# Another order of work in the opening of a fused attention and feed-forward kernel

## The chip, the cores and the metric

The kernel runs on one core of one Trainium2 chip. A core has five engines with their own instruction queues: TensorE (PE: matmuls, and the loading of their weights as PEld), VectorE (DVE), ScalarE (ACT), GpSimd (POOL) and SyncE (SP, which here only issues DMAs); POOL and ACT issue DMAs too. Each engine takes its instructions strictly in order and waits on semaphores for the others. The metric is the device time of one execution in microseconds (us).

## The reference

The reference is attention over four batches, eight heads, 768 positions and 64 numbers a head, followed by a feed-forward network (FFN) with a maximum over three products. Five of the heads keep only the first four keys and a window of 64 keys ("streaming" heads), three keep all keys up to the position ("retrieval" heads); which ones is an input.

```
scores = scale * q @ k.T                       # per batch and head, 768 x 768
mask   = causal                if is_retrieval[h]
         causal & (sink|window) otherwise
a      = softmax(where(mask, scores, -1e9))
x      = (a @ v), heads side by side           # 3072 x 512
h      = max(max(x @ w1, x @ w2), x @ w3)      # 512 -> 768
out    = h @ w_out                             # 768 -> 512
```

## The kernel before

**Units of work.** A batch is cut into two halves of 384 query rows, and its heads, in the order `HEADS`, into two groups of four. One tile `t` is one half and one group: `t = 4*batch + 2*half + group`. A tile has two pairs of heads, `i` = 0 and 1. The FFN is cut into 21 units for each half batch: 18 sums (three weights by six blocks of 128 columns, each four matmuls of 384 columns) and three output blocks.

**An order written out by hand.** No scheduler orders the instructions. Three long lists of items, `FIRST` (line 62), `NEAR` (line 75) and `ANY` (line 118), are read from left to right, and each item calls one function (the table `do`, near the end of the kernel function) that puts its instructions on the queues of the engines concerned. What stands earlier in a list stands earlier on every queue that it uses. `FIRST` is the opening: it ends with `av`s and transposes of batch 0's first half. Then a branch on the input flags takes `NEAR` where the retrieval heads are the ones that the kernel knows, or `ANY` where they are others; with this input it is `NEAR` (its masks `NM`, line 565, are in the trace, and only `NEAR` makes them).

**The items that matter here.** The last letter names the engine of a copy: `a` ACT, `d` DVE, `p` POOL.
- `hl half pair n which s`: SP loads a pair of heads of batch 0's k (which = 0) or q (1) in a half. `load_v`: loads v. SP's list of DMAs is in one order before and after.
- `cast half pair which e` (line 335): turns such a load to 16 bit, into one of three buffers `kn` or `qn`.
- `turnp half pair ee` (lines 362 and 378): PE transposes six blocks of 128 columns into one or two PSUM banks; the named engines copy them to the tile `KQ`.
- `em pair`: two DVE instructions (line 599) that write the mask of two heads, for the early scores; `flags` and `read` bring the flags into place, `far` the factors of distant keys.
- `s t u [i]`: scores. PE adds the mask (line 851, in tiles 0 and 1) and the products (line 876) into a score buffer `st` (two of them) or, with `b`, into two banks, and ACT takes the exponential (line 887) into `pt`.
- `v t i e` (line 730) casts v; `vp half n e` (lines 747 and 750) puts its rows in order by three matmuls of 512 columns and a copy; `vf` (line 762) scales it.
- `av t i` (lines 964, 977 and 979): the product with v into a bank; DVE takes the reciprocal of the sums and writes `x`. `x t i e` (lines 998 and 1002) transposes it for the FFN as `xT`.
- `w 0 2 part`: POOL issues three DMAs (line 619) with half of the weight w1 (the tile `w0t`). `load b g`: POOL issues four DMAs (line 389) with k and q of a batch; `turn b g which part` (line 407) is a DVE transpose of a quarter of that load.
- `f 1 e`: the next FFN unit, with its copy, if it has one, on engine `e`; maxima are always on DVE (line 673).
- `idle n`: PE computes n empty products of 512 columns (line 484) into a score buffer that nobody reads. `number`: each engine reads the branch flag (line 1061).
- `k`, `c`, `kc`: masks on `pt` after the exponential, and joins of the first keys with the window's.

**Buffers.** There are four PSUM banks of the general kind, taken in turn by `turnp`, `vp`, `av`, `x`, `f` and by scores with `b`; the fifth user waits until the first one's bank is read. There are two `st`, taken in turn. The lines that decide this:

```
sps = turns("sps", 2, space=bass.MemoryType.PSUM)
bkp = turns("bkp", 4, space=bass.MemoryType.PSUM)

def run(program):
    for line in program:
        for item in line.split(", "):
            name, *args = item.split()
            do[name](*args)
```

Of the kernel before, what the change touches and what calls it, by code (L numbers as in the profile page):

```python
# [59 lines left out]


FIRST = (
# [10 lines left out]
)  # L73
# [42 lines left out]
)  # L116

ANY = (
# [1029 lines left out]
```

## Time and profile before

| | before |
|---|---|
| time, median of 3 runs | 189.58 us (189.18 to 189.71) |
| the profiled execution's own time | 190.51 us |
| its span | 188.7 us |
| PE busy | 181.1 us (96%) |
| DVE, ACT, POOL busy | 140.3 (74%), 103.6 (55%), 85.7 us (45%) |
| first FFN matmul of a real unit | 23.05 us after the span's start |
| PE's longest wait after that | 0.73 us, at 76.8 us |

A busy share is the time in which an engine has an instruction under way. In the timeline each row has the start, the time that the row covers, the engine, the line, the operation, its tiles and how many instructions were merged (x3); in brackets stands how long the engine had been idle and what ended the wait. "bank" is any of the four PSUM banks. PE's rows start when the first matmul of the group enters, and matmuls overlap: successive ones of 384 columns start some 0.16 us apart at the full clock.

### The profile page before, as it was taken

To read this page: it belongs to the slowest core of one execution; us is meant where nothing else is said; L and a number is where in the kernel's file an instruction comes from. 1 tells how busy PE (TensorE), PEld (TensorE's weight loads), DVE (VectorE), ACT (ScalarE), POOL (GpSimd) and SP (SyncE) were. 2 spreads that over 40 slices of the span, in tenths; PEclk is the share of its full clock that TensorE was granted. 3 is DMA by queue.
4 is the path that set the end of the run, shared out by engine and by line. 5 is a ranking of instruction groups with operands and counts; after the bars stand their busy time and mean duration, and the time that the engine had idled before them with its cause. 6 is when DMAs were issued, how large, how long until landed. Compare 5 with 4: busy or idle time off the path is not lost. (4 is left out here: it accounts for less than half of the span.)

```text
span 188.7 us, 4937 instructions
## 1 busy us (share of the span) xinstructions
PE 181.1 (96%) x1930; PEld 104.6 (55%) x1930; DVE 140.3 (74%) x297; ACT 103.6 (55%) x164; POOL 85.7 (45%) x121
## 2 busy tenths in 40 slices
PE   7989999999999999799999999999999999999992
PEld 2446646555565555375556565664656456746552
DVE  3739999999869996999899868773658357834740
ACT  4488999442676994548585548545245534123022
POOL 6258989600569797069302286059922402000000
PEclk9999999999999999999999999999999999999998
DMA  4999999995999999972999541211212220332004
GB/s 129 266 349 280 171 196 209 205 202 118 227 184 246 183 198 229 247 63 53 206 259 192 91 167 24 42 26 67 105 21 45 86 102 2 66 95 94 7 0 167
DMA packets 43180, 26.49 MB, mean 140 GB/s; under 512 B 30866, under 2 KB 38674, under 8 KB 43154
## 3 DMA queue, kind: packets, MB, share of 16 engines
q1 hardware_dynamic: 37794, 18.03, 39.3%
q0 software_dynamic: 4944, 7.87, 24.7%
q8 instruction: 15, 0.25, 0.5%
q10 hardware_dynamic: 416, 0.26, 0.4%
q14 instruction: 11, 0.09, 0.2%
HBM read 25.17 MB, written 6.29 MB: 167 GB/s over the span
## 5 line engine op out<-in xcount | busy, mean ns | idle before, releaser
L887 ACT ACTIVATE pt<-st 128x1024 f16<-128x1024 f32 (+2 forms) x72 | 63.0, 927 | 27.9 <-PE st L876 22.8
L648 PE MATMUL bank<-xT,w1t 128*128 128x384 f16 x180 | 35.7, 326 | 0.7 <-DVE acc L673 0.7
L648 PE MATMUL bank<-xT,w2t 128*128 128x384 f16 x180 | 36.0, 326 | 0.0
L673 DVE TENSOR_TENSOR acc<-bank,acc 128x384 f16<-128x384 f32 x45 | 24.9, 556 | 14.9 <-PE bank L648 12.4
L648 PE MATMUL bank<-xT,w0t 128*128 128x384 f16 x180 | 35.7, 326 | 0.2 <-DVE hT L673 0.2
L908 POOL TENSOR_TENSOR pt<-pt,NM 128x1024 f16<-128x1024 f16 (+2 forms) x14 | 26.6, 1910 | 11.2 <-ACT pt L887 10.4
L668 ACT CAST acc<-bank 128x384 f16<-128x384 f32 x33 | 15.5, 485 | 29.2 <-PE bank L648 28.8
L692 PE MATMUL bank<-woutt,hT 128*128 128x512 f16 (+1 forms) x138 | 30.7, 372 | 0.0
L673 DVE TENSOR_TENSOR hT<-bank,acc 128x384 f16<-128x384 f32 x45 | 24.5, 556 | 4.7 <-PE bank L648 2.1
L407 DVE STREAM_TRANSPOSE KQ<-kq 128x384 f32<-128x384 f32 x24 | 25.8, 1129 | 1.6 <-DMA kq<-in_k_dram 1.6
L648 PEld LDWEIGHTS <-w0t 128*128 128x128 f16 x192 | 17.9, 98 | 12.9 <-issue 1.3
L648 PEld LDWEIGHTS <-w1t 128*128 128x128 f16 x192 | 17.6, 98 | 12.5 <-issue 1.3
L926 POOL TENSOR_TENSOR pt<-pt,mk 128x512 f16<-128x512 f16 (+1 forms) x12 | 12.9, 1080 | 25.2 <-ACT pt L887 24.7
L648 PEld LDWEIGHTS <-w2t 128*128 128x128 f16 x192 | 17.4, 98 | 11.2 <-issue 0.4
L692 PEld LDWEIGHTS <-hT 128*128 128x128 f16 x156 | 14.4, 98 | 15.4 <-issue 0.3
L964 PEld LDWEIGHTS <-pt 128*128 128x128 f16 x492 | 18.6, 97 | 4.2 <-issue 0.8
L876 PE MATMUL st<-KQ 32*128 32x128 f16 (+4 forms) x468 | 20.8, 255 | 0.0
L964 PE MATMUL bank<-va,pt 128*128 128x65 f16 x409 | 19.9, 193 | 0.0
L979 DVE TENSOR_TENSOR x<-bank,rc 128x384 f16<-128x384 f32 x32 | 17.8, 558 | 1.1
L876 PEld LDWEIGHTS <-KQ 32*128 32x128 f16 (+1 forms) x472 | 9.6, 93 | 13.0 <-issue 10.2
L698 ACT COPY ot<-bank 128x512 f32<-128x512 f32 (+1 forms) x15 | 8.4, 568 | 14.0 <-PE bank L692 12.6
L784 POOL COPY KC<-KQ 128x256 f32<-128x256 f32 x4 | 1.6, 392 | 18.5 <-DVE KQ L407 18.5
(109 smaller groups left out, 186.4 us busy)
## 6 DMA issues: line engine op xcount, KB each, us to landing
out_dram<-ot SPq DMA_DIRECT2D x23, 256.0 KB, 2.0
vs<-in_v_dram SPq DMA_DIRECT2D x18, 256.0 KB, 6.0
kq<-in_k_dram POOLq DMA_DIRECT2D x6, 288.0 KB, 6.0
kq<-in_q_dram POOLq DMA_DIRECT2D x6, 288.0 KB, 8.1
qs<-in_q_dram SPq DMA_DIRECT2D x6, 192.0 KB, 5.0
ks<-in_k_dram SPq DMA_DIRECT2D x6, 192.0 KB, 4.6
vs<-in_v_dram SPq DMA_DIRECT2D x2, 384.0 KB, 6.4
vs<-in_v_dram SPq DMA_DIRECT2D x1, 768.0 KB, 5.7
```

Source lines behind the costliest of these rows:

```text
L407: nc.vector.transpose(out=dst.rearrange("c (p j) -> c j p", j=n)[:, j0:j1], in_=src.rearrange("c (j i) -> c j i", i=R),)
L648: nc.tensor.matmul(yy[:, 0:HALF], w_t[wi][:, ks, ni * P : (ni + 1) * P], xT[b, half, ks].rearrange("p a t -> p (a t)"), start=(ks == 0), s ...
L668: copy_out[0](out=acc[ni], in_=yy[:, 0:HALF])
L673: nc.vector.tensor_tensor(out=dst, in0=yy[:, 0:HALF], in1=acc[ni], op=ALU.max)
L692: nc.tensor.matmul(yo[:, 0:n], hT[ns][:, tb * P : (tb + 1) * P], woutt[:, ns, c : c + n], start=(ns == 0), stop=(ns == NNB - 1),)
L698: op(out=ot[:, c : c + n], in_=yo[:, 0:n])
L876: nc.tensor.matmul(sts[x][:, c0 : c0 + n * P], keys, KQ[rows, 1, t0 : t0 + n * P], start=(c0 == 0 and r == 0 and not early), stop=(b == 0 ...
L887: nc.scalar.activation(out=pts[t, i][:, u, m0:m1, 0:w], in_=sts[i, m0][:, 0:w].unsqueeze(1) if apart else sts[i][:, :, 0:w], func=AF.Exp, ...
L908: engine.tensor_tensor(out=x, in0=x, in1=m, op=ALU.mult)
L926: engine.tensor_tensor(out=x, in0=x, in1=m, op=ALU.mult)
L964: nc.tensor.matmul(o[:, qi, hl, 0 : D + 1], pt[:, u, hl, c : c + P], vv[:, 0 : D + 1], start=(idx == 0), stop=(idx == len(todo) - 1), skip ...
L979: nc.vector.tensor_tensor(out=x, in0=o[:, :, :, 0:D], in1=rc.unsqueeze(3).to_broadcast([P, HB, 2, D]), op=ALU.mult,)
```

## The change

It touches only the three lists.

In `FIRST`:
- Empty products: 2 + 8, 3, 2 and 2 become 2 + 6, 3 and 2.
- The masks are written in the order of pairs 0, 3, 2, 1 instead of 1, 0, 3, 2, with transposes' copies between them.
- ACT's copies of `turnp 0 0` stand before `cast 0 3 1 a` instead of behind it. One copy of `turnp 0 3` goes from ACT to DVE.
- `s 0 0 0` stands before `turnp 0 3` and before `cast 0 2 0 a`. `s 1 1 1` and `s 1 1 0` stand before the v placements `vp 0 1` and `vp 0 0`, and `s 1 1 1` also before `cast 0 1 0 a`.
- `v 0 0` goes from POOL to DVE, `cast 1 2 1` from DVE to POOL.
- `number` and `w 0 2 0` stand before POOL's `cast 1 1 0` and `cast 1 1 1` instead of behind them.
- `turnp 1 1` stands behind `vp 0 2` and `s 0 0 1` instead of ahead of them; `turnp 1 0` and `cast 1 3 1 a` stand behind `s 0 0 1` too.

In `NEAR` the item `turn 2 1 0 1` goes five items back, behind `vf 8 0 d, c 2 0 0 d, k 6 0 2 d, s 8 0, f 1 d`. The rest is the same items, wrapped in other lines. `ANY`, which this input does not run, gets `idle 8, idle 2` at its start.

```diff
 FIRST = (
-    "read, idle 2, hl 0 2 2 1 s, hl 0 2 2 0 s, differ, cast 0 0 0 a, idle 8, flags, cast 0 2 1 p",
-    "em 1, load_v 0 0 4 4, load_v 0 0 0 4, cast 0 3 0 p, v 1 1 p, cast 0 0 1 a, cast 0 3 1 a",
-    "turnp 0 0 aa, hl 0 1 1 1 s, far, hl 1 0 2 0 s, v 1 0 p, idle 3, v 0 0 p, cast 0 2 0 a, em 0",
-    "hl 0 1 1 0 s, turnp 0 3 da, idle 2, cast 1 0 0 p, cast 0 1 1 p, em 3, hl 1 0 2 1 s, s 0 0 0",
-    "em 2, turnp 0 2 ad, s 0 1 0 b, v 0 1 d, idle 2, s 1 0 1, s 1 0 0, cast 0 1 0 a, vp 0 1 d",
-    "vp 0 0 d, cast 1 1 0 p, cast 1 1 1 p, cast 1 0 1 d, hl 1 2 2 1 s, s 1 1 1, hl 1 2 2 0 s",
-    "s 1 1 0 b, turnp 0 1 a, cast 1 3 1 a, vf 0 0 d, load_v 0 1, number, w 0 2 0, vf 0 1 d",
-    "vf 1 1 d, vf 1 0 d, turnp 1 1 d, cast 1 2 1 d, vp 0 2 a, turnp 1 0 da, load 1 0, s 0 0 1",
+    "read, idle 2, hl 0 2 2 1 s, hl 0 2 2 0 s, differ, cast 0 0 0 a, idle 6, flags, cast 0 2 1 p",
+    "load_v 0 0 4 4, load_v 0 0 0 4, cast 0 3 0 p, v 1 1 p, cast 0 0 1 a, turnp 0 0 aa",
+    "cast 0 3 1 a, hl 0 1 1 1 s, em 0, far, em 3, hl 1 0 2 0 s, v 1 0 p, idle 3, s 0 0 0",
+    "cast 0 2 0 a, hl 0 1 1 0 s, turnp 0 3 dd, em 2, s 0 1 0 b, idle 2, cast 1 0 0 p",
+    "cast 0 1 1 p, hl 1 0 2 1 s, turnp 0 2 ad, em 1, s 1 0 1, v 0 1 d, v 0 0 d, s 1 0 0, s 1 1 1",
+    "cast 0 1 0 a, s 1 1 0 b, hl 1 2 2 1 s, hl 1 2 2 0 s, load_v 0 1, number, vp 0 1 d, vp 0 0 d",
+    "w 0 2 0, turnp 0 1 a, vp 0 2 a, cast 1 1 0 p, cast 1 1 1 p, cast 1 0 1 d, vf 1 0 d, vf 0 0 d",
+    "vf 0 1 d, vf 1 1 d, s 0 0 1, turnp 1 1 d, turnp 1 0 da, cast 1 3 1 a, cast 1 2 1 p, load 1 0",
     "cast 1 3 0 p, av 1 0, v 2 1 p, av 0 0, s 0 1 1, s 2 0 1, av 1 1, av 0 1, v 3 0 d, v 2 0 d",
     "x 1 0 a, s 2 0 0",
 )
...
 NEAR = (
...
-    "load 2 1, k 5 1 2 p, f 1 a, f 1 d, k 6 1 1 p, f 1 a, f 1 a, turn 2 1 0 1, vf 8 0 d",
-    "c 2 0 0 d, k 6 0 2 d, s 8 0, f 1 d, av 7 1 D, load 3 0, turn 2 1 1 0, f 1 a, f 1 a",
+    "load 2 1, k 5 1 2 p, f 1 a, f 1 d, k 6 1 1 p, f 1 a, f 1 a, vf 8 0 d, c 2 0 0 d, k 6 0 2 d",
+    "s 8 0, f 1 d, turn 2 1 0 1, av 7 1 D, load 3 0, turn 2 1 1 0, f 1 a, f 1 a, k 6 1 0 p, f 1 d",
...
 ANY = (
-    "rest, cast 1 2 0 p, m 1, x 0 0 a, s 2 2 1, x 0 1 d, w 0 2 1, s 2 3 0, s 2 2 0, k 2 1 1 d",
+    "rest, idle 8, idle 2, cast 1 2 0 p, m 1, x 0 0 a, s 2 2 1, x 0 1 d, w 0 2 1, s 2 3 0",
...
```

49 rows, old and new, of tables (ANY, NEAR) are left out of this document.

## The prediction

> **What bounds the kernel now.** I read the page's busy times first, then PE's waits, then the timeline of each engine in the two stretches that the change touches.
>
> ```profile
> PE 181.1 (96%) x1930; PEld 104.6 (55%) x1930; DVE 140.3 (74%) x297; ACT 103.6 (55%) x164; POOL 85.7 (45%) x121
> ...
> PE st L484 <- DVE zero L476: 1.3, 1, 1.3
> PE bank L648 <- DVE acc L673: 0.7, 1, 0.7
> PE bank L747 <- POOL kq L730: 0.7, 1, 0.7
> ```
>
> PE is the bound. From the first FFN matmul (23.05 us) to 176 us it waits noticeably in one place, near 77 us. So the time moves with two things: when PE gets to that first FFN matmul, and what that one place costs. In the opening PE's busy share means little, because empty products are counted; there the chain across engines decides.
>
> ```profile
> 13.38 0.50 POOL L335 CAST kn<-ks 128x384 f16<-128x384 f32 x1 [0.61 <-ACT pt L887]
> 13.82 0.50 POOL L335 CAST qn<-kq 128x384 f16<-128x384 f32 x1
> 14.27 0.50 POOL L335 CAST kn<-ks 128x384 f16<-128x384 f32 x1
> 14.97 0.50 POOL L335 CAST qn<-qs 128x384 f16<-128x384 f32 x1 [0.20 <-DMA qs<-in_q_dram]
> 16.12 2.11 POOL L619 DMA_DIRECT2D w0t<-in_moe_w_dram  x3 [0.65 <-DVE qn L335]
> ...
> 13.89 0.51 ACT L335 CAST kn<-kq 128x384 f16<-128x384 f32 x1 [0.56 <-DMA kq<-in_k_dram]
> ...
> 16.07 0.49 PE L362 MATMUL bank<-ident,qn 128*128 128x128 f16 x6 [0.38 <-issue]
> 16.66 0.96 DVE L378 COPY KQ<-bank 128x768 f16<-128x768 f16 x1 [0.26 <-ACT KQ L378]
> 18.45 0.41 PE L964 MATMUL bank<-va,pt 128*128 128x65 f16 x8
> 23.05 0.81 PE L648 MATMUL bank<-xT,w0t 128*128 128x384 f16 x4
> ...
> 75.40 1.13 DVE L407 STREAM_TRANSPOSE KQ<-kq 128x384 f32<-128x384 f32 x1 [1.58 <-DMA kq<-in_k_dram]
> 76.92 0.53 DVE L673 TENSOR_TENSOR acc<-bank,acc 128x384 f16<-128x384 f32 x1
> 77.50 0.81 PE L648 MATMUL bank<-xT,w1t 128*128 128x384 f16 x4 [0.73 <-DVE acc L673]
> 79.62 0.81 PE L648 MATMUL bank<-xT,w0t 128*128 128x384 f16 x4 [0.21 <-DVE hT L673]
> ```
>
> See: POOL does four casts in a row and then stands for 2.11 us on three DMA issues; ACT's cast at 13.89 waits for its load; PE's six transposes at 16.07 are `turnp 1 1`, and DVE's copy of 0.96 follows. The last four rows are one story: DVE waits for a load with a maximum queued behind it, and PE waits for that maximum's bank.
>
> **The opening up to ACT's cast of k.** Two empty products fewer at the start are 2 x 0.427 us (4.45 us hold ten, started 0.427 apart), so PE is free at 4.7 instead of 5.5. The flags then wait for DVE's last flag row (4.77 + 0.15): 5.0 instead of 5.64, 0.65 gained. The first transposes follow, and ACT copies them at 5.7 to 6.55 instead of 6.70 to 7.56, as `cast 0 3 1` (6.29 for 0.51) is no longer ahead. The first mask pair is the needed one and is ready at 6.2. Three empty products hold PE until 6.9, then `s 0 0 0`: its exponential starts at about 7.9 instead of 9.41. Then the lead melts: `cast 0 2 0` is now behind that exponential (8.85 instead of 8.54), `turnp 0 2` waits for it until 9.4, and the exponential of `s 1 0 1` comes at 11.1 instead of 11.40. With 0.92 each for that and `s 1 0 0`, then 0.60 for `s 1 1 1`, ACT is done at 13.55 and waits for the load, cast at 13.89 as before. Everything gained so far is worth nothing, and the two remaining empty products saved (2 x 0.216), the copy moved to DVE (0.59) and `v 0 0` (0.5 on POOL, 0.36 on DVE) lie ahead of the same wait. SP's order is unchanged; its loads wait for landings, not for the casts that move.
>
> **From there to the first FFN matmul.** ACT saves the 0.60 of `s 1 1 1` and 0.35 of waiting. PE has the scores behind it at 13.4, reads the flag (0.54, the gap before 16.07), places v with six products (6 x 0.216 = 1.3), transposes `turnp 0 1` (6 x 0.056), places three more (0.65) and does `s 0 0 1` (0.75, from 17.38 to 18.13 in the rows): 17.0. Next is `turnp 1 1`, which needs POOL's `cast 1 1 1`. On POOL `cast 1 0 0` still waits for its load (13.38) and `cast 0 1 1` ends at 14.32. If the 0.65 before the first w0 issue stays, it starts at 14.97 instead of 16.12; 2.08 of issues (16.12 to 18.21), then two casts (0.45 + 0.50): 18.0 instead of 15.47. PE stands 0.9 us. The transposes end at 18.4, DVE's copy is done at 18.5 + 0.96 = 19.45 (17.62 before). `turnp 1 1` now holds the bank that `av 0 0` gets next, so `av 0 0` starts at 19.5 instead of 18.45: 1.05 later. From `av 0 0` to the first FFN matmul the order is unchanged and takes 23.05 - 18.45 = 4.6. So that matmul comes at 24.1, +1.05.
>
> Behind it: POOL takes over a cast (0.45), so the second w0 half is issued at about 21.4 instead of 21.11; it is used first by the fourth FFN unit, at 28.7 before and 1.05 later now, with the landing 0.3 later: hidden. v's second half shares the DMA engines with w0 from 15.5 on; its first cast was at 20.66, queued behind POOL's issues, and moves to 20.9: hidden as well. PE has no idle time left that could take up the 1.05.
>
> Bounds. Above: if the masks or a late clock also push ACT past 13.89, some 0.3 more: +1.35. Below: if the 0.65 is not paid again, w0 starts at 14.33, `cast 1 1 1` ends at 17.4, the copy at 18.85, and the loss is 0.45. If issues held POOL for nothing, `turnp 1 1` could go at 17.05, its copy would end at 18.4, and `av 0 0` would be where it was: 0. I take 1.05, as the 0.65 is in the row of the very instruction that moves.
>
> A rule to weigh here is in the Trainium skill, page "SBUF — State Buffer", summary of port rules: a VectorE copy or cast between SBUF tiles may lock GpSimd's port, and DMAs issued from GpSimd then cannot write descriptors. By it the 0.65, which the row lays to DVE's cast of qn (14.94 to 15.50), would vanish, since at 14.33 DVE has no such cast, and the sum would be 0.45. Against the rule, the wait outlasts that cast by 0.6 us, and the third w0 issue ran beside the DVE cast at 17.54 in 0.61 us.
>
> **The place at 77 us.** In the new order DVE goes on at 73.81 (73.25 + 0.56) with 0.26 + 0.17 + 0.40 us of small work, waits for PE's sum (74.28 + 0.82 = 75.1), and does the maximum at 75.15. The transpose starts at 75.6; its load landed before 75.40. PE's bank is free at 75.7, before PE wants it (76.62), so the 0.73 goes. DVE's chain then runs from 75.6 where it ran from 75.40 with all four jobs (1.5 us) behind it: the reciprocal at 76.55 instead of 77.38, the next `hT` about 0.8 earlier, and PE's row at 79.62 moves to about 78.85. Gain 0.8; bounds 0.94 (both of PE's waits) and 0 (DVE is over 90% busy from 75 to 100 us and could take it back).
>
> **Sum.** +1.05 - 0.8 = +0.25. Span 188.7 becomes 188.9, that execution's 190.51 becomes 190.8; it stood 0.93 above the median of 189.58, so the median goes to 189.8. A measurement of this kernel can tell about 0.3%, 0.57 us, from no change (189.0 to 190.2).
>
> **The rivals.**
> - Slower: the gain at 77 us does not come. Place: DVE behind 79 us, full in the slices there; price: the 0.8; it decides once the PE row that waits for hT still follows the first FFN matmul by 56.6 us as before. For it: DVE's digits of 9; against: DVE gains 1.1 us of its own empty time. Time 189.58 + 1.05 = 190.6. With the upper bound of the opening, or loads slowed by w0, 190.9 or more.
> - The 0.65 is not paid: 0.45 - 0.8 = -0.35: 189.2.
> - POOL's issues don't hold its casts, so the change does not delay what I say: 0 - 0.8, 188.8; with 0.2 to 0.5 from the flag read hidden, 188.4. Against: POOL's cast at 20.21 came only when seven issues were through.
> - Fewer empty products leave PE at half clock one stretch longer. The Trainium skill, page "TensorE: Matmul & The Clock Gate", Part 1, says the full clock comes after about 3.4 us of sustained work, counted in windows of their own. The rows show 0.427 us a product up to 5.1 and 0.216 from 6.7 on; at half speed up to 9.9, PE's work there would take 1 us more, of which ACT's wait at 13.89 leaves at most 0.3. It is part of the upper bound.
>
> **How the numbers follow.** Forecast, around 189.8: 0.34 (0.22 within 0.3%, 0.10 slower, 0.02 faster). Gain at 77 us missing, 190.6: 0.20 (0.18 slower). Opening worse as well, 190.9 to 191.5: 0.14 (0.13 slower). The 0.65 gone, 189.2: 0.20 (0.13 within, 0.07 faster). POOL not held, 188.8 or less: 0.12 (0.11 faster). Together: faster 0.20, same 0.39, slower 0.41. The likeliest case alone reaches from 189.3 to 190.3. The range to 8 in 10 cuts half of the two outer cases: 188.7 to 191.0.
>
> **What would show it.** First exponential near 7.9 us; ACT's cast of k still at 13.9; w0's first issue at 15.0 and POOL's second cast behind it at 18.0; PE idle ahead of six transposes near 17 us; first FFN matmul at 24.1; no wait over 0.3 us behind DVE's maximum near 77 us, and no transpose of DVE waiting for a load. It is wrong if POOL's casts come before 17 us, if PE's order there hides them, or if the later rows keep their distance from the first FFN matmul.

## The result, and the profile after

The changed kernel takes 190.6 us in the median (189.92 to 191.95, 15 executions) against 189.54 us for the kernel before beside it (188.2 to 190.95): a ratio of 1.0075, 95% interval 1.0048 to 1.0103. It is slower, by 0.9 to 1.95 us. Medians are over all executions; ratios leave out those more than 1.5% above the fastest of the same kernel, and need not be the quotient of two medians. The profiled execution took 190.03 us with a span of 188.2 us. The forecast was 189.8, called no measurable change; the range held the result, and the place where the loss arises was right, but a gain that was to pay for most of it did not come.

All line numbers of the changed kernel are one lower than before. First PE's list of waits; its columns are what waited for what, the us in total, how often, and the longest. (Of the three lines shown of before, only `L484 <- DVE zero` has an equal here.)

```profile
PE st L483 <- DVE zero L475: 1.3, 1, 1.3
PE bank L361 <- POOL qn L334: 1.0, 2, 0.7
PE bank L361 <- ACT kn L334: 0.9, 1, 0.9
PE bank L963 <- DVE KQ L377: 0.5, 1, 0.5
...
PE bank L647 <- DVE hT L672: 0.4, 1, 0.4
```

`POOL qn` and `DVE KQ` ahead of L963 are new: PE waits for the cast that stands behind w0's issues, and then, with `av 0 0`, for DVE's copy behind that cast. The `DVE acc` wait of 0.7 near 77 us is gone, and the one for `hT` is 0.4 instead of 0.2. The rows of the opening, from the timelines of POOL, ACT, PE and DVE in turn:

```profile
12.77 0.50 POOL L334 CAST kn<-ks 128x384 f16<-128x384 f32 x1 [1.02 <-DMA ks<-in_k_dram]
13.21 0.50 POOL L334 CAST qn<-kq 128x384 f16<-128x384 f32 x1
14.05 2.12 POOL L618 DMA_DIRECT2D w0t<-in_moe_w_dram  x3 [0.33 <-issue]
16.14 0.54 POOL L334 CAST kn<-ks 128x384 f16<-128x384 f32 x1
16.63 1.01 POOL L334 CAST qn<-qs 128x384 f16<-128x384 f32 x2
...
6.65 1.02 ACT L886 ACTIVATE pt<-st 128x1024 f16<-128x1024 f32 x1
13.28 0.51 ACT L334 CAST kn<-kq 128x384 f16<-128x384 f32 x1
...
17.19 0.34 PE L361 MATMUL bank<-ident,qn 128*128 128x128 f16 x3 [0.74 <-POOL qn L334]
18.70 0.34 PE L963 MATMUL bank<-va,pt 128*128 128x65 f16 x6 [0.47 <-DVE KQ L377]
23.24 0.81 PE L647 MATMUL bank<-xT,w0t 128*128 128x384 f16 x4
...
15.66 2.13 DVE L761 TENSOR_TENSOR vf<-va,far 128x128 f16<-128x128 f16 x4
17.71 1.45 DVE L377 COPY KQ<-bank 128x768 f16<-128x768 f16 x2
```

POOL turns to w0 two casts earlier than before; the two casts of half 1 follow at 16.14 and 16.63. PE's transposes of `turnp 1 1` stop in the middle for 0.74, DVE copies from 17.71, and `av 0 0` starts at 18.70. The absolute times hide the loss, because in this execution the loads landed earlier: the first FFN matmul is at 23.24, only 0.19 behind the 23.05 of before, but ACT's second cast of k, which stands at about the time its load lands, is at 13.28 instead of 13.89. From that cast to the first FFN matmul it is 23.24 - 13.28 = 9.96 us; before, 23.05 - 13.89 = 9.16. This distance is the measure of the opening below.

The place at 77 us, from the timelines of DVE and PE:

```profile
75.43 0.56 DVE L672 TENSOR_TENSOR acc<-bank,acc 128x384 f16<-128x384 f32 x1 [0.33 <-PE bank L647]
75.91 1.12 DVE L406 STREAM_TRANSPOSE KQ<-kq 128x384 f32<-128x384 f32 x1
...
76.82 0.81 PE L647 MATMUL bank<-xT,w1t 128*128 128x384 f16 x4
79.12 0.81 PE L647 MATMUL bank<-xT,w0t 128*128 128x384 f16 x4 [0.38 <-DVE hT L672]
```

The maximum now comes ahead of the transpose, and `w1t` follows without a wait. From the first FFN matmul to the row that waits for hT it is 55.88 us, where it was 56.57. So against the first profile of before a gain is there: 0.69. The second measure below is the whole remaining distance, the remainder: the span less the time of the first FFN matmul, 188.7 - 23.05 = 165.6 before, 188.2 - 23.24 = 165.0 after. From the row that waits for hT to the end it is 109.1 us in both, so all of this difference arises ahead of that row. Opening 0.8 longer and remainder 0.7 shorter would be no change. But the times say +1.06 in the medians. The experiments had to settle which of the two profiles is the odd one.

### The profile page after: what moved, and what is told of

Read it like the earlier page. It is cut to its first block, busy times and chain, and to the rows that moved or that the text cites. A ratio compares the mean times of both kernels' runs of the same rounds, so it can differ in the third digit from the quotient of the medians.

```text
span 188.2 us, 4927 instructions
## 1 busy us (share of the span) xinstructions
PE 179.6 (95%) x1926; PEld 103.8 (55%) x1926; DVE 140.5 (75%) x298; ACT 103.3 (55%) x163; POOL 85.5 (45%) x121
## 5 line engine op out<-in xcount | busy, mean ns | idle before, releaser
L963 PEld LDWEIGHTS <-pt 128*128 128x128 f16 x492 | 18.7, 97 | 4.6 <-issue 1.1
L963 PE MATMUL bank<-va,pt 128*128 128x65 f16 x409 | 20.0, 193 | 0.5 <-DVE KQ L377 0.5
```

The source lines that it names most:

```text
L963: nc.tensor.matmul(o[:, qi, hl, 0 : D + 1], pt[:, u, hl, c : c + P], vv[:, 0 : D + 1], start=(idx == 0), stop=(idx == len(todo) - 1), skip ...
```

## Experiments

**The changed kernel once more.** No edit.

> The changed kernel once more, beside runs of the kernel before on the same chip, with the span of every run. Theory A (the opening reaches the first FFN matmul later and the place at 77 us gives 0.7 back): the spans differ by +0.2 to +0.5 us, and the times by the same. Theory B (the loss lies outside of what the two profiled executions showed: the profiled spans were 188.2 against 188.7 while the medians were 190.6 against 189.5): times differ by +1 us or more, and either the time around the span is larger, or the profiled executions were not typical ones.

Measured: 190.72 us, ratio 1.0046 (1.0014 to 1.0078) to a before of 189.46. In this execution the loads landed later: ACT's cast at 13.94, the first FFN matmul at 23.92. The distance is 9.98, the remainder 188.9 - 23.92 = 165.0. Both measures repeat to 0.02, while the absolute times moved by 0.7. The loss is real, and Theory B holds: over all executions the median span is 188.7 against 187.5 before, so the first profile of before, with 188.7, was a long one.

**The moved transpose alone.** The kernel before, with

```diff
-    f 1 a, f 1 a, turn 2 1 0 1, vf 8 0 d, c 2 0 0 d, k 6 0 2 d, s 8 0, f 1 d, av 7 1 D
+    f 1 a, f 1 a, vf 8 0 d, c 2 0 0 d, k 6 0 2 d, s 8 0, f 1 d, turn 2 1 0 1, av 7 1 D
```

> The kernel before with the one move in NEAR alone: the transpose behind the five items. Theory A: PE's wait of 0.73 us near 77 us is gone and the later PE row keeps 55.9 us instead of 56.6 from the first FFN matmul; 0.7 us faster (ratio 0.996). Theory B: no gain in time, as what PE wins is taken back later (ratio 1.000).

Measured: 189.47 us, ratio 0.9997 (0.9965 to 1.0029). The predicted 0.8 us would be a ratio of 0.9958, outside the interval. On average the move is worth nothing that this interval (0.7 us faster to 0.5 us slower) can show: Theory B for the time. Its reason, that the gain is taken back later, is another matter: in this profile too it is 109.0 us from the row that waits for hT to the end.

**The new opening alone.** The kernel before with the changed list `FIRST`, and the transpose in its old place.

> The kernel before with the new FIRST alone; NEAR and ANY as before. Theory A: first FFN matmul 0.2 to 1.05 us later and the wait of 0.73 near 77 us still there: +0.2 to +1.05 us, so 0.7 us slower than the changed kernel. Theory B: the whole measured loss of 1 to 1.4 us, or more, is in FIRST whatever the place at 77 us does, and this kernel is no slower than the changed one.

Measured: 190.24 us, ratio 1.0034 (1.0000 to 1.0068), beside the changed kernel's 1.0046, so no slower than it as far as these intervals show: Theory B. The opening is 23.31 - 13.27 = 10.04. This execution has the old place of the transpose, and its timelines of DVE and PE there show no trouble:

```profile
74.23 1.14 DVE L407 STREAM_TRANSPOSE KQ<-kq 128x384 f32<-128x384 f32 x1 [0.16 <-DMA kq<-in_k_dram]
...
76.87 0.81 PE L648 MATMUL bank<-xT,w1t 128*128 128x384 f16 x4
78.62 0.81 PE L648 MATMUL bank<-xT,w0t 128*128 128x384 f16 x4
```

The transpose waits 0.16 us instead of 1.58, PE not at all, and the remainder is 187.7 - 23.31 = 164.4: 1.2 shorter than in the first profile of before and 0.6 shorter than with the moved transpose. The last row stands 78.62 - 23.31 = 55.31 behind the first FFN matmul, where it was 56.57 with the wait for the load and 55.88 with the moved transpose, and from there to the end it is 109.1 as in the others. So with the load in time the old place is the better one, by 0.57; with the load late the moved one is better, by 0.69.

**The kernel before once more.** No edit.

> The kernel before, unchanged, profiled once more. The profiled execution of before was 1.1 us longer than its usual span of 187.5 us. Theory A (the wait of 0.73 us near 77 us belonged to that one execution, whose load landed late): span near 187.5, the first FFN matmul about 9.1 us behind the start of ACT's second cast of k (13.89 in the first profile), no transpose of DVE near 75 us that waits over 0.3 us for its load, and no wait of PE over 0.3 us there. Rival B (the wait is in the order of the kernel before, and its gain was taken back elsewhere): the transpose waits 1.0 us or more again and PE 0.5 us or more.

Measured in one execution: 189.67 us, span 187.9. The opening is 22.38 - 13.22 = 9.16, exactly as in the first profile, but the first FFN unit is broken here: its other three matmuls start at 22.93 and the next unit comes 0.39 later than in the first profile, which goes into the remainder. The transpose of 77 us starts at 74.51 and waits for nothing. Theory A holds for that place, with a reserve: DVE comes to it 52.13 behind the first FFN matmul, where it was 50.92 with the new opening alone, so the delays ahead of it may have covered a late landing. But another load was late here, that of the quarter at 66 us, and cost PE 0.43 (timelines of DVE and PE):

```profile
66.01 1.13 DVE L407 STREAM_TRANSPOSE KQ<-kq 128x384 f32<-128x384 f32 x1 [1.79 <-DMA kq<-in_k_dram]
...
72.83 0.81 PE L648 MATMUL bank<-xT,w2t 128*128 128x384 f16 x4 [0.43 <-DVE acc L673]
```

Which load of batch 2 is late changes from execution to execution. It is not a property of the order of before: in both profiles of the changed kernel DVE waited for the load of 66 us too, for 1.40 and 1.61, and there PE did not wait.

**The changed kernel with w0 behind POOL's casts.**

```diff
-    w 0 2 0, turnp 0 1 a, vp 0 2 a, cast 1 1 0 p, cast 1 1 1 p, cast 1 0 1 d
+    turnp 0 1 a, vp 0 2 a, cast 1 1 0 p, cast 1 1 1 p, w 0 2 0, cast 1 0 1 d
```

> The changed kernel with the three issues of w0's first half put back behind POOL's casts 1 1 0 and 1 1 1. Theory A (those casts behind 2.1 us of issues hold PE): the casts end some 2 us earlier, PE's wait of 0.74 ahead of turnp 1 1 and of 0.47 ahead of av 0 0 go, and the first FFN matmul comes 0.4 to 0.8 us earlier than in the changed kernel: ratio to before about 1.003 or less. Theory B (the loss has another cause): as slow as the changed kernel, 1.0075.

Measured: 189.65 us, ratio 0.9984 (0.9955 to 1.0014). The loss is gone: Theory A. The profiled execution had a wait of 4.02 us for a load at 67.85 us, so only its opening is read: 22.53 - 13.69 = 8.84. The same kernel once more:

> The changed kernel with w0's three issues behind POOL's two casts, once more, for a trace of an ordinary execution and more times. Theory A: first FFN matmul 8.85 us behind ACT's second cast of k (9.1 to 9.2 before, 9.96 in the changed kernel), POOL's second cast of half 1 done within 1.2 us of its first cast behind the load, no wait of PE for POOL's casts; time 189.3 to 189.7. Rival B (the other moves of the opening cost something too, hidden by chance in the first measurement): 189.9 or more.

Measured: 189.73 us, ratio 1.0014 (0.9982 to 1.0046), opening 22.01 - 13.26 = 8.75. Its timelines of POOL and PE:

```profile
13.21 0.50 POOL L336 CAST qn<-kq 128x384 f16<-128x384 f32 x1
13.66 0.50 POOL L336 CAST kn<-ks 128x384 f16<-128x384 f32 x1
14.36 0.50 POOL L336 CAST qn<-qs 128x384 f16<-128x384 f32 x1 [0.20 <-DMA qs<-in_q_dram]
14.93 2.12 POOL L620 DMA_DIRECT2D w0t<-in_moe_w_dram  x3
...
15.84 0.51 PE L363 MATMUL bank<-ident,qn 128*128 128x128 f16 x6
17.47 0.34 PE L965 MATMUL bank<-va,pt 128*128 128x65 f16 x6 [0.41 <-DVE KQ L379]
```

The casts end 1.65 us behind the 13.21 of the one ahead of them (14.86), where in the changed kernel the second one ends 3.92 behind it (17.13); the six transposes run in one piece. The opening is now 0.3 to 0.4 shorter than before, yet the time is the same within the intervals: 0.3 is less than they can show. Its profiled execution has a remainder of 166.6, with PE waits of 0.67 and 0.43 behind two late loads.

**w0 ahead, alone.** The kernel before, with one item moved (`number`, the read of the flag, stays where it was):

```diff
-    cast 1 1 0 p, cast 1 1 1 p, ..., number, w 0 2 0, vf 0 1 d
+    w 0 2 0, cast 1 1 0 p, cast 1 1 1 p, ..., number, vf 0 1 d
```

> The kernel before with one item moved: w0's three issues stand ahead of POOL's two casts of half 1, as in the changed kernel; all else as before. Theory A (those issues hold the casts, and that is the loss): w0 starts at about 14.6 us where the casts ended at 14.77, lasts 2.1, and the cast that the six transposes need ends at about 17.6 instead of 15.47; the transposes come 1.6 us later than 16.07, DVE's copy ends 1.2 to 1.5 later, and so does the first FFN matmul. Time 190.6 to 191.1 against 189.5. Rival B (the loss comes from the new places of the transposes, the factors and the copies on DVE): no loss here, 189.5 within 0.3.

Measured: 190.93 us, ratio 1.0074 (1.0045 to 1.0102) to a before of 189.23. The opening is 24.10 - 13.77 = 10.33, 1.17 longer; A's 1.2 to 1.5 was slightly too much. Timelines of POOL, PE and DVE:

```profile
14.05 2.12 POOL L619 DMA_DIRECT2D w0t<-in_moe_w_dram  x3
16.14 0.63 POOL L335 CAST kn<-ks 128x384 f16<-128x384 f32 x1
16.72 0.50 POOL L335 CAST qn<-qs 128x384 f16<-128x384 f32 x1
...
17.27 0.34 PE L362 MATMUL bank<-ident,qn 128*128 128x128 f16 x3 [1.07 <-POOL qn L335]
...
78.63 0.81 PE L648 MATMUL bank<-xT,w1t 128*128 128x384 f16 x4 [0.74 <-DVE acc L673]
...
76.53 1.13 DVE L407 STREAM_TRANSPOSE KQ<-kq 128x384 f32<-128x384 f32 x1 [1.59 <-DMA kq<-in_k_dram]
```

One item costs as much as the whole change: Theory A. And the waits in the rows at 76.53 and 78.63, 1.59 and 0.74, are those of the first profile of before, to 0.01: the load of 77 us was late again, with a remainder of 189.8 - 24.10 = 165.7 against 165.6 there. So the late case is not unique; it is one of the ways in which an execution can go.

**The wait that remains.** In the kernel with w0 behind, `av 0 0` still waits 0.41 for DVE's copy. So the transposes were put ahead of the score unit, and two factor products behind the copies:

```diff
-    vf 1 0 d, vf 0 0 d, vf 0 1 d, vf 1 1 d, s 0 0 1, turnp 1 1 d, turnp 1 0 da
+    vf 1 0 d, vf 0 0 d, turnp 1 1 d, s 0 0 1, turnp 1 0 da, vf 0 1 d, vf 1 1 d
```

> The changed kernel with w0 behind POOL's two casts, and besides the six transposes of half 1 ahead of the score unit s 0 0 1, and two of DVE's four factor products behind its two copies. Theory A (what is left in the opening is the 0.41 us that the second product with v waits for DVE's copy): that wait goes, the first FFN matmul comes 0.3 to 0.4 us earlier than with w0 behind alone, 8.4 to 8.5 us behind ACT's second cast of k, and the time is 189.0 to 189.2 against 189.5 for the kernel before. Rival B (the opening's lead is given back later, at loads that land when they land): first FFN earlier, time 189.4 to 189.6.

Measured: 189.78 us, ratio 1.0027 (1.0000 to 1.0053); the opening 22.83 - 13.54 = 9.29, 0.5 longer instead of 0.4 shorter. The expectation missed. `av 0 0` waits no longer, but two other waits are there, in the timelines of PE and ACT:

```profile
16.08 0.51 PE L363 MATMUL bank<-ident,qn 128*128 128x128 f16 x6 [0.28 <-DVE qn L336]
21.67 0.34 PE L999 MATMUL bank<-ident,x 128*128 128x128 f16 x3 [0.35 <-DVE x L980]
...
17.29 1.02 ACT L888 ACTIVATE pt<-st 128x1024 f16<-128x1024 f32 x1 [0.81 <-PE st L877]
```

The transposes wait for DVE's cast of q, the score unit stands behind them, and ACT's exponential for it, which ran at 15.95 in the kernel with w0 behind, now waits 0.81 and starts at 17.29. The score unit behind the transposes is the worse order here; the two factor products moved with it, so the 0.5 is the price of both moves. With the moved transpose and loads in time the remainder is 187.8 - 22.83 = 165.0 again.

**Loads earlier, in the old order.** The opening with w0 behind, the transpose in its old place, and

```diff
-    k 5 1 1 p, f 1 a, f 1 d, v 7 0 a, av 5 1 D, load 2 0, f 1 d
+    load 2 0, k 5 1 1 p, f 1 a, f 1 d, v 7 0 a, av 5 1 D, f 1 d
...
-    c 1 1 1 p, turn 2 0 1 1, ..., load 2 1, k 5 1 2 p
+    load 2 1, c 1 1 1 p, turn 2 0 1 1, ..., k 5 1 2 p
```

> The new opening with w0 behind POOL's two casts, the main list of before (so without the moved transpose), and in it two loads issued earlier: load 2 0 ahead of the mask k 5 1 1 on POOL (some 2 to 4 us earlier), load 2 1 ahead of the join c 1 1 1 (0.8 us earlier). Theory A (in the old order the transposes of batch 2 cost PE time only when their load lands late): no transpose of DVE between 60 and 80 us waits over 0.3 us for a load, the end comes 164.2 to 164.6 us behind the first FFN matmul (164.35 where the load was in time, 165.6 where it was late), and with the opening 0.3 us shorter the time is 188.6 to 189.0 against 189.4 before. Rival B (the loads' lead is lost again, as their packets share the DMA engines with others): distance 165 or more, time 189.2 to 189.6.

> The kernel with the new opening, w0 behind POOL's casts, the old place of the transpose and the two loads issued earlier, once more. Theory A (opening 0.3 us shorter, and the waits for late loads gone): 0.4 to 0.9 us below the kernel before, ratio 0.995 to 0.998. Rival B (the first measurement was a favourable chance): ratio 0.999 to 1.001.

Measured: 189.24 us, ratio 0.9966 (0.9932 to 1.0000), and the second time 190.05, ratio 1.0011 (0.9970 to 1.0052). DVE's transposes, from the timeline of the first of the two:

```profile
63.80 1.12 DVE L408 STREAM_TRANSPOSE KQ<-kq 128x384 f32<-128x384 f32 x1
65.81 2.07 DVE L408 STREAM_TRANSPOSE KQ<-kq 128x384 f32<-128x384 f32 x2
70.18 1.12 DVE L408 STREAM_TRANSPOSE KQ<-kq 128x384 f32<-128x384 f32 x1
73.44 1.13 DVE L408 STREAM_TRANSPOSE KQ<-kq 128x384 f32<-128x384 f32 x1
```

None waits for a load, in this execution or in the second, as expected; the remainder is 164.8 and 164.9, not the 164.4 that was expected, and the opening is 8.74 both times. But the two ratios together do not show that this kernel is faster than the one before. In the second execution most of the missing 0.4 stands at one place, in its timelines of DVE and PE:

```profile
57.63 1.96 DVE L909 TENSOR_TENSOR pt<-pt,NM 128x1024 f16<-128x1024 f16 x1
...
60.11 1.46 PE L649 MATMUL bank<-xT,w2t 128*128 128x384 f16 x8 [0.35 <-DVE acc L674]
```

That mask took 1.45 with the new opening alone, and the maximum behind it came later for it. Why it took longer is not shown. In the first execution PE has no wait over 0.2 from the first FFN matmul to 82 us; the 0.4 is spread over smaller pieces.

**The load later, in both orders.** In the kernel before, and in the kernel with the moved transpose alone:

```diff
-    load 2 1, k 5 1 2 p, f 1 a, f 1 d, k 6 1 1 p
+    k 5 1 2 p, load 2 1, f 1 a, f 1 d, k 6 1 1 p
```

> The kernel before with load 2 1 issued one item of POOL later, behind the mask k 5 1 2 (about 1.6 us later). Theory A (what the moved transpose saves is a wait for a late landing): DVE's transpose near 76 us waits 1.5 us or more in every execution, PE behind it 0.7 to 2.3, the end comes 165.7 to 167.5 us behind the first FFN matmul; time 0.8 to 2.3 above before. Rival B (a late landing doesn't reach PE): 189.4 within 0.3.

> As the run with load 2 1 issued later, but with the transpose 2 1 0 1 five items back, as in the changed kernel. Theory A (the move is worth something only where the landing is late): 0.6 to 1.3 us faster than the run with the later load and the old order, the end 0.6 to 1.3 us nearer to the first FFN matmul. Rival B (the move is worth nothing in any case): the same time as that run within 0.3.

Measured: old order 191.48 us, ratio 1.0072 (1.0039 to 1.0106); moved transpose 193.08 us, ratio 1.0065 (1.0022 to 1.0108). In the old order a load issued 1.8 us later (68.51 instead of 66.72) costs 1.4 us by the ratio: a late landing does reach PE. The rows of DVE and PE:

```profile
65.74 1.13 DVE L407 STREAM_TRANSPOSE KQ<-kq 128x384 f32<-128x384 f32 x1 [1.42 <-DMA kq<-in_k_dram]
...
76.25 1.13 DVE L407 STREAM_TRANSPOSE KQ<-kq 128x384 f32<-128x384 f32 x1 [1.15 <-DMA kq<-in_k_dram]
...
73.33 0.81 PE L648 MATMUL bank<-xT,w2t 128*128 128x384 f16 x4 [0.42 <-DVE acc L673]
78.35 0.81 PE L648 MATMUL bank<-xT,w1t 128*128 128x384 f16 x4 [0.53 <-DVE acc L673]
```

DVE waits 1.15 near 76 us where 1.5 or more was expected, and PE 0.53 where it was 0.7 or more. The row at 73.33 belongs to the load of 66 us (DVE's row at 65.74), whose issue did not move and which was late here as well; so the remainder of this profile, 166.5, is not the price of the later issue alone.

The comparison of the two orders is inconclusive: the two intervals overlap almost entirely, and that of the moved transpose rests on six executions. That the move helps where this load is late was not measured. It is argued from rows: with loads in time the moved transpose starts 75.91 - 23.24 = 52.67 behind the first FFN matmul (75.53 - 22.83 = 52.70 in the run with the transposes first), and the late loads of before and of w0 ahead let theirs start at 52.35 and 52.43. A load as late as those would not hold the moved one.

## Why the prediction was right or wrong

The three distances of the profiles, in us; the second ends at the row of `w0t` that waits for hT near 79 us, or would:

| | ACT's cast to first FFN matmul | from there to the row for hT | from there to the end of the span |
|---|---|---|---|
| before, twice | 9.16, 9.16 | 56.57, 56.51 | 165.6 (load of 77 us late), 165.5 (load of 66 us late) |
| moved transpose alone | 9.07 | 56.27 | 165.3 (load of 66 us late) |
| new opening alone | 10.04 | 55.31 | 164.4 (loads in time) |
| after, twice | 9.96, 9.98 | 55.88, 55.89 | 165.0, 165.0 (no wait of PE behind a load) |
| before, w0 ahead | 10.33 | 56.65 | 165.7 (load of 77 us late) |
| after, w0 behind, twice | 8.84, 8.75 | not read, 57.53 | not read, 166.6 (two loads late) |
| the same, transposes first | 9.29 | 55.91 | 165.0 (loads in time) |
| w0 behind, old place, loads earlier, twice | 8.74, 8.74 | 55.76, 55.82 | 164.8, 164.9 (loads in time) |

The last column less the one before it is 109.0 to 109.1 in every row: whatever these kernels differ by arises ahead of that row.

- **The opening up to ACT's cast: right in its worth, not in every row.** The first exponential started at 6.65 in the first profile of the changed kernel and at 7.84 in the second, where 7.9 was forecast, and in both ACT came to its cast of k straight from other work, not from a wait. Still nothing was gained by it: the cast starts at 13.58 in the mean of six profiles with the old opening (13.22 to 13.93) and at 13.54 in the mean of eight with the new one (13.26 to 13.94). The copy moved to DVE, the masks and the empty products together are worth nothing up to this point, as forecast.
- **From there to the first FFN matmul: right.** Forecast +1.05; measured 9.96 - 9.16 = 0.80, 0.82 and 0.88. Each link of the chain was there: w0 ahead, casts late, transposes stopped (0.74 of the forecast 0.9), copy late, `av 0 0` waiting for its bank (5.42 behind ACT's cast instead of 4.56, so +0.86). The mis-sized term is the 0.65 ahead of the first w0 issue. It was taken as a price of that issue. The trace's register instructions show what it is: POOL's read of the flag, the item `number`. In the profile of before it runs for 0.50 from 14.98, beside POOL's last cast, and the issue starts 0.65 after its end. In the changed kernel it runs from 12.90, and the issue at 14.05 again starts 0.65 after its end; but a cast fills half of that time, and 0.33 of idle is left. With w0 alone moved ahead and `number` left behind, w0 starts at 14.05 with no gap. What fills the 0.65 behind the read is not shown. The rule weighed against the row, of the Trainium skill, page "SBUF — State Buffer", was therefore not put to the test: the gap shrank, but not for its reason.
- **The place at 77 us: the step that failed.** "Gain 0.8" was read off one execution. There the rows were right, and the same rows before and after give 0.69. But the wait of 1.58 for a landing, from which the 0.73 of PE followed, is not in every execution: of the four profiles of the old order with its loads where they were, two have it (the first of before, w0 ahead) and two have not. With the load in time the old order has no wait there, and the moved transpose adds the one for hT (0.38) and costs 0.57. So the move gains 0.69 or loses 0.57, by the landing of one load, and alone it measured 0.9997. A sign stood in the numbers at hand: the profiled execution lay 0.93 above the median, and the prediction noted it and carried it through instead of asking which of its rows made it longer.
- **The rival with the right time had the wrong reason.** 190.6 was forecast for "the gain at 77 us does not come", with DVE taking it back behind 79 us. Its own test was that the row waiting for hT would still follow the first FFN matmul by 56.6; it follows by 55.88. Nothing was taken back later: from that row to the end it is 109.0 to 109.1 in every order. The gain was missing because the move also has a price, which every execution with its load in time pays.
- **The other rivals.** POOL's issues do hold its casts, and the changed order does what it says. The clock came late in some executions and not in others: behind the flags the three empty products ran 0.21 us apart from 5.14 on in the first profile of the changed kernel, and still 0.43 apart from 5.51 on in the second. It had no price here, as ACT's cast behind the first exponential still waited for its load in both, 0.97 at 8.65 and 0.50 at 9.36.

That the range held the result is owed to its width: the sum missed by 0.8, the size of the gain that did not come. Sum in place of the forecast one: +0.85 in the opening, 0 in the mean at 77 us. On the median of 189.54 that is 190.4, just under the first interval (190.45 to 191.49); on the 189.46 of the second measurement it is 190.3, inside its interval (189.7 to 190.9). If something of 0.1 or 0.2 us is missing, these runs don't show it. The w0 issues are the cause of the loss: without them ahead the time is that of before, twice, and with them alone the loss is there.

## What to carry to other kernels

Before a DMA issue is moved forward on an engine that also computes, list what stands behind it on that queue: here three issues of together 2.1 us held two casts of 0.5 us, for which PE, DVE and a PSUM bank were waiting. A wait for a DMA landing in one profile is no standing cost: take a second profile, or ask whether the profiled execution was longer than its median by just that wait. And a move that shortens such a wait can cost something in the executions that have none; price both. Compare traces by distances between events of the same work and not by absolute times, when the first loads can land 0.7 us earlier or later.

## What the runs showed of the hardware

- Four factor products on DVE (`vf`, two operands in SBUF, 0.28 us for one) take 0.89 to 1.01 us in nine profiles in which w0's issues stand behind POOL's casts (in four of these POOL issues w0's DMAs all the while), but 2.13, 1.64 and 1.65 us in the three profiles of the changed opening, in which casts of POOL run beside them. In the changed kernel single ones took 1.03 and 0.58 from 16.24 on, beside POOL's casts from 16.14. The Trainium skill, page "SBUF — State Buffer", section "SBUF: two separate sides", says that a VectorE operation with two SBUF inputs and a GpSimd operation that reads SBUF exclude each other by a lock; these rows agree only in part, since in each of the three profiles the first product took 0.41 to 0.46 before POOL's first cast began, while POOL's rows show nothing but w0's issues. It cost little here: in the other two profiles DVE then still waited 0.36 and 0.86 for PE's transposes, and only in the first did the factors end just where the copy began.
- POOL's next DMA issue follows the end of its read of the branch flag by 0.64 to 0.65 us in all eight profiles in which at most one cast stands between them, whether that cast fills part of the time or not.
- In the kernel before, with no change, the loads of batch 2 land so differently that DVE's wait for them at one place, near 66 us, is 0 in one profile and 1.79 us in the other.
